# A two-layer strided convolution with a joint head on one core: a new schedule for the leading 254 columns

## Chip, cores, metric

The kernel runs on one core of one Trainium2 chip. The metric is device time of one execution in microseconds (us), median over several executions. The span that the profile shows is about 1.8 us shorter than the time that the same execution reports. Every run in this document was in the fast state. All kernels gave a correct result.

Ratios are computed as the mean time of one kernel's runs over the mean time of the other's runs of the same rounds, so they are not quite the ratio of the medians that are quoted beside them.

## The reference

```python
B, T, D, K = 2, 4000, 512, 5;  U = 8          # all bfloat16
xp = pad(x, 2 columns of zeros at both ends of T)
h = gelu(sum_i xp[:, i:i+T, :] @ w1[i])[:, ::2, :]        # layer 1, 5 taps, stride 2
hp = pad(h, 2 at both ends)
f = gelu(sum_i hp[:, i:i+T1, :] @ w2[i])[:, ::2, :]       # layer 2, 5 taps, stride 2
fe = f @ w_f;  ge = g @ w_g
j = tanh(fe[:, :, None, :] + ge[:, None, :, :])
return j @ w_o                                            # (2, 1000, 8, 512)
```

## The kernel before

Columns are split into four phases (column modulo 4), so both parities of a strided output read whole phases. Layer 1 of batch 0 is cut into three tiles: a leading tile (columns 0 to 249), tile 1 (250 to 499) and tile 2 (500 to 999, 500 wide). Every tile has four groups of 128 output channels, m = 0 to 3. A "tap" is one of the five convolution weights.

The leading tile is computed tap by tap: 5 taps x 4 groups x 2 parities x 4 contraction steps = 160 matmuls. All other tiles use minimal filtering: seven products (b2, a1, a2, a0, b1, b3, a3) of *transformed* operands give both parities, 28 matmuls a group in place of 40. The price is work on other engines: ScalarE copies a phase shifted by one column, VectorE subtracts and adds phases and sums weights (wsum), and each group has a post-processing, a "post" below (ScalarE scales one bank, VectorE combines, ScalarE applies gelu).

```python
CELL = 32            # bytes; dependencies are tracked per cell of this size
...
def xf(src, off, dst, c0, n, which):                  # transforms on VectorE
    ph = lambda r: src[r, :, off:off + n]
    o = lambda kind: dst[kind, :, c0:c0 + n]
    if which == "a0":   tt("dve", o(0), o(0), ph(2), sub)  # o(0): ScalarE's shifted copy
    elif which == "a3": tt("dve", o(2), o(2), ph(0), sub)
    elif which == "b1": tt("dve", o(3), o(3), ph(1), sub)
    elif which == "b3": tt("dve", ph(3), ph(3), ph(1), sub)      # in place
    elif which == "a1": tt("dve", o(1), ph(0), ph(2), add)
    elif which == "a2": tt("dve", ph(0), ph(2), ph(0), sub)      # in place
...
count = {"unit": 2}
...
    def banks(self, m):                               # PSUM: 8 banks of 512 columns
        if self.n <= 256:                             # two banks a group
            base = (count["unit"] % 4) * 2 * NT
            ...
        else:                                         # four banks a group
            base = (count["unit"] % 2) * 4 * NT
            ...
        count["unit"] += 1
...
for i in (0, 4, 2, 1, 3):                             # leading tile, all by taps
    for m in range(NK):
        for s in range(2):
            r, d = tap_at[i][s]
            mm(ps.cols(m * NT + 256 * s, n),
               [(w1_sb[i, k, m*P:(m+1)*P], xs[0][r, k, 16+d:16+d+n]) for k in range(NK)], ...)
for m in range(NK):
    wsum04(w1_sb, w1_t, "dve", m)
wsum13(w1_sb, w1_t, "dve")
...
for w in ("a0", "b1", "a3"):                tiles[1].shift(w)   # ScalarE
for w in ("a0", "b1", "b3", "a3", "a1", "a2"): tiles[1].xf(w)   # VectorE
...
for qi in range(1, len(tiles)):
    ...
    for m in range(NK):
        where = tile.products(m)
        ...
        if qi == 6 and m == 0:
            ge()                                      # small gate product, PSUM bank 0
            fe(0)
```

`CELL` belongs to the program's own planner, not to the chip: the planner makes an engine wait wherever two accesses touch the same cell.

The loads: x for the leading tile (two blocks, "turned", that is transposed, on TensorE) and then transposing loads on SyncE's queue, the five weight taps on ScalarE's queue.

## Time and profile before

| | before |
|---|---|
| time, median of the first three runs | 292.46 us (292.26 to 292.56) |
| time of the run that was profiled | 293.93 us |
| TensorE busy | 280.4 of 292.1 us (96%) |
| chain that ended last | 92% TensorE |
| VectorE, ScalarE busy | 62%, 54% |

TensorE is the bottleneck, so what counts is where it stands still or runs slowly. The waits view of the kernel before lists who kept TensorE waiting (total us, times, longest us):

```profile
PE acc L302 <- DVE ty_67 L291: 2.6, 1, 2.6
PE acc L302 <- DVE xt_54 L291: 2.0, 1, 2.0
PE acc L302 <- POOL warm L288: 1.3, 1, 1.3
PE acc L302 <- DVE ty_69 L291: 1.3, 1, 1.3
PE acc L302 <- issue: 1.2, 1, 1.2
```

The second and the first line are the gaps before tile 1 (27.2 to 29.2 us) and before tile 2 (43.0 to 45.6 us). The timeline of the same kernel shows what was happening in them; the columns are start, duration, engine, line, operation, output and inputs, shape, count, and in brackets the idle time just before and what ended it:

```profile
27.33 0.68 DVE L291 TENSOR_TENSOR xs_49<-xs_49 128x1000 bf16<-128x1000 bf16 x1 [6.99 <-PE acc L302]
...
29.25 1.00 PE L302 MATMUL acc<-xs_49,w_t 128*128 128x250 bf16 x4 [2.02 <-DVE xt_54 L291]
...
43.78 1.19 DVE L291 TENSOR_TENSOR xs_50<-xs_50 128x2000 bf16<-128x2000 bf16 x1
44.89 0.67 DVE L291 TENSOR_TENSOR ty_67<-ty_67,acc 128x500 f32<-128x500 f32 x1
...
45.62 1.15 PE L302 MATMUL acc<-xs_50,w_t 128*128 128x500 bf16 x4 [2.58 <-DVE ty_67 L291]
```

VectorE stood idle for 7.0 us until the last tap matmul was done; then it did three transforms and tile 1 could start. Before tile 2, TensorE waited for the end of VectorE's sum into ty_67, the last post-processing of tile 1.

Windows of 2 us of the same kernel follow: stretch, its length, then busy us and instruction count of TensorE, its weight loads, VectorE, ScalarE and GpSimd, then the granted TensorE clock (1.00 is full speed), the share of the DMA engines and GB/s.

```profile
28.00:30.00 2.00, 0.76 (x4) 0.57 (x5) 1.87 (x4) 0.00 (x0) 0.00 (x0) 0.83 0.95 199
30.00:32.00 2.00, 2.00 (x12) 1.44 (x10) 0.00 (x0) 0.06 (x1) 0.00 (x0) 0.50 1.64 221
...
46.00:48.00 2.00, 2.00 (x7) 0.80 (x6) 0.00 (x0) 0.00 (x0) 0.00 (x0) 0.59 1.22 161
48.00:50.00 2.00, 2.00 (x7) 0.70 (x5) 0.00 (x0) 1.53 (x3) 0.00 (x0) 0.55 1.83 244
```

After each of the two gaps the granted clock falls, to 0.50 in 30 to 32 us and to 0.59 and 0.55 in the two windows from 46 us: TensorE is "busy" all the time, but in 30 to 32 us it starts 12 matmuls of 250 columns where a full-clock window holds about 21.

### The profile page before, as it was taken

The page shows a single profiled execution, that of the slowest core. Times are in us where ns is not written, and L with a number is a line of the kernel's source. Part 1 is how long each engine was busy: PE and PEld are TensorE (multiplying, and loading weights), DVE is VectorE, ACT ScalarE, POOL GpSimd, SP SyncE. Part 2 cuts the span into 40 slices and gives each one's busy share as a digit, 9 for nine tenths or more (in the row PEclk, how much of TensorE's full clock was granted, in tenths as well). Part 3 has the DMA queues.
Part 4 walks back from the last instruction along what each step waited for, and adds up shares of the span by engine and source line. Part 5 has one row for each costly group of instructions (what it writes and reads, how often), then busy time and mean ns, then how long its engine had stood idle before and what let it go on. Part 6 is the DMA issues. An engine that isn't in the chain of part 4 may idle for free.

```text
span 292.1 us, 3892 instructions
## 1 busy us (share of the span) xinstructions
PE 280.4 (96%) x1460; PEld 141.6 (48%) x1460; DVE 182.3 (62%) x237; ACT 158.0 (54%) x187; POOL 33.1 (11%) x39
## 2 busy tenths in 40 slices
PE   8897987999999999999989999999999999999995
PEld 3796873444444444444434444444444444444442
DVE  0872493687598668576633346566757576666764
ACT  2333653722842662563315628667886785975930
POOL 1000000099994000000000000000000000000000
PEclk9999797999999999999999999999999999999999
DMA  7999939990000000000000002244454444444444
GB/s 267 320 205 222 208 74 164 319 312 0 3 0 0 0 2 0 0 2 0 0 0 2 0 1 74 68 147 161 142 167 145 156 151 154 153 148 159 145 148 138
DMA packets 54575, 31.85 MB, mean 109 GB/s; under 512 B 31630, under 2 KB 54302, under 8 KB 54558
## 3 DMA queue, kind: packets, MB, share of 16 engines
q1 hardware_dynamic: 51918, 28.99, 36.6%
q10 hardware_dynamic: 2640, 2.62, 2.7%
q8 instruction: 11, 0.18, 0.3%
q14 instruction: 6, 0.05, 0.1%
HBM read 7.86 MB, written 16.38 MB: 83 GB/s over the span
## 4 chain that ended last, share of the span: by engine, by line
PE 92%; DVE 3%; issue 2%; ACT 1%; POOL 0%; DVEq 0%; ACTq 0%; POOLq 0%
PE acc L302 92%; ACT xt_55 L295 1%; DVE ty_69 L291 1%; PE acc L363 1%; DVE xt_54 L291 0%; DVE xt_55 L291 0%; DVE ty_68 L486 0%; DVE ost_86 L626 0%; DVE ty_67 L291 0%; DVE ty_68 L291 0%; DVE ty_69 L486 0%; DVE ty_67 L486 0%; POOL zero L288 0%; ACT cs_65 L295 0%; ACT cs_66 L295 0%
## 5 line engine op out<-in xcount | busy, mean ns | idle before, releaser
L302 PE MATMUL acc<-wo_sb,jT 128*128 128x512 bf16 x500 | 108.2, 379 | 0.0
L302 PEld LDWEIGHTS acc<-wo_sb,jT 128*128 128x128 bf16 x500 | 48.9, 98 | 59.0
L302 PE MATMUL acc<-xt_55,w_sb 128*128 128x500 bf16 x160 | 38.3, 374 | 0.0
L295 ACT ACTIVATE jT<-feT_80,geT 128x1000 bf16<-128x1000 f32 (+6 forms) x44 | 35.8, 890 | 0.0
L295 ACT ACTIVATE jT<-feT_79,geT 128x1000 bf16<-128x1000 f32 (+4 forms) x40 | 35.1, 949 | 0.0
L302 PE MATMUL acc<-xt_54,w_sb 128*128 128x500 bf16 (+1 forms) x160 | 33.8, 347 | 0.0
L295 ACT ACTIVATE cs_65<-acc 128x500 f32<-128x500 f32 (+1 forms) x12 | 6.6, 553 | 37.8 <-PE acc L302 37.8
L302 PE MATMUL acc<-xs_49,w_sb 128*128 128x250 bf16 (+1 forms) x192 | 23.7, 278 | 1.2 <-issue 1.2
L302 PEld LDWEIGHTS acc<-xt_55,w_sb 128*128 128x128 bf16 x160 | 15.7, 98 | 18.4 <-issue 0.5
L302 PEld LDWEIGHTS acc<-xt_54,w_sb 128*128 128x128 bf16 x160 | 16.0, 100 | 13.4
L302 PEld LDWEIGHTS acc<-xs_49,w_sb 128*128 128x128 bf16 x192 | 18.6, 97 | 4.8 <-issue 1.3
L295 ACT ACTIVATE cs_66<-acc 128x500 f32<-128x500 f32 (+1 forms) x12 | 6.6, 552 | 25.2 <-PE acc L302 25.2
L302 PE MATMUL acc<-xs_49,w_t 128*128 128x250 bf16 (+1 forms) x64 | 13.6, 339 | 2.0 <-DVE xt_54 L291 2.0
L295 ACT ACTIVATE ost_93<-acc 128x512 bf16<-128x512 f32 x10 | 6.0, 597 | 16.4 <-PE acc L302 16.4
L626 DVE CAST ost_82<-acc 128x512 bf16<-128x512 f32 x11 | 7.6, 691 | 10.3 <-PE acc L302 10.3
L626 DVE CAST ost_88<-acc 128x512 bf16<-128x512 f32 x10 | 6.9, 692 | 10.3 <-PE acc L302 10.3
L291 DVE TENSOR_TENSOR ty_69<-ty_69,acc 128x1000 f32<-128x1000 f32 (+1 forms) x8 | 9.0, 1128 | 6.2 <-PE acc L302 6.2
L291 DVE TENSOR_TENSOR ty_68<-ty_68,acc 128x1000 f32<-128x1000 f32 (+1 forms) x8 | 9.0, 1128 | 6.1 <-PE acc L302 6.1
L295 ACT ACTIVATE ost_87<-acc 128x512 bf16<-128x512 f32 x10 | 5.9, 593 | 11.4 <-PE acc L302 11.4
L302 PE MATMUL acc<-xs_50,w_t 128*128 128x500 bf16 x32 | 9.0, 406 | 2.6 <-DVE ty_67 L291 2.6
L291 DVE TENSOR_TENSOR ty_67<-ty_67,acc 128x1000 f32<-128x1000 f32 (+1 forms) x8 | 8.5, 1060 | 4.1 <-PE acc L302 4.1
L486 DVE SCALAR_TENSOR_TENSOR ty_68<-acc,cs_65 128x500 f32<-128x500 f32 x8 | 5.1, 674 | 7.4 <-PE acc L302 7.4
(116 smaller groups left out, 362.4 us busy)
## 6 DMA issues: line engine op xcount, KB each, us to landing
w_sb<-in_w_dram ACTq DMA_DIRECT2D x5, 512.0 KB, 8.4
w_sb<-in_w_dram SPq DMA_DIRECT2D x5, 512.0 KB, 6.4
out_dram<-ost_82 SPq DMA_DIRECT2D x11, 128.0 KB, 1.9
out_dram<-ost_86 SPq DMA_DIRECT2D x11, 128.0 KB, 1.8
out_dram<-ost_84 SPq DMA_DIRECT2D x10, 128.0 KB, 1.8
out_dram<-ost_90 SPq DMA_DIRECT2D x10, 128.0 KB, 1.9
out_dram<-ost_83 SPq DMA_DIRECT2D x9, 128.0 KB
out_dram<-ost_85 SPq DMA_DIRECT2D x9, 128.0 KB
```

Source lines behind the costliest of these rows:

```text
L291: pl.op(eng, lambda e: e.tensor_tensor(out=o.ap, in0=a.ap, in1=b.ap, op=op), (a, b), (o,))
L295: pl.op("act", lambda e: e.activation(o.ap, i.ap, func, scale=scale, bias=0.0 if bias is None else bias.ap), rd, (o,))
L302: ins = e.matmul(o.ap, lhsT=l.ap, rhs=r.ap, start=start and n == 0, stop=stop and n == len(pairs) - 1, skip_group_check=not check)
L363: ins = e.transpose(pv.ap[:, r, k, :], xr[rt].h[:, 2 * pp + r, k, :], ident.h[:, :])
L486: pl.op("dve", lambda e, o=o, f=f: e.scalar_tensor_tensor(out=o.ap, in0=d.ap, scalar=f, in1=c.ap, op0=ALU.mult, op1=add), (d, c), (o,))
L626: pl.op("dve", lambda e, o=o, v=v: e.tensor_copy(out=o.ap, in_=v.ap), (v,), (o,))
```

## The change

As described, it takes the leading columns (254 now) with two channel groups tap by tap and two by minimal filtering; all loads go through one queue, x first, then the taps, then the transposing loads; and the products that read phase 0 come last in the first group of a tile. The core of it, condensed (dots mark cuts, and some lines are joined or commented by me):

```diff
-CELL = 32
+CELL = 4
-    NWARM = 16
+    NWARM = 12
...
-        for i in (0, 4, 2, 1, 3):
-            load_w("act", w1_sb[i], ...)
+        for i in (0, 1, 3, 4, 2):
+            load_w1("sp", i)                 # after the two x blocks, same queue
...                                           # turning: phases 0/2 of both blocks first
+            if which == "a0" and keep:       # leading tile: nothing in place, no shift for a0
+                tt("dve", o(0), src[2, :, off - 1:off - 1 + n], ph(2), sub)
...
-                tt("dve", ph(0), ph(2), ph(0), sub)
+                tt("dve", ph(2), ph(2), ph(0), sub)          # a2 in place in phase 2
...
-        count = {"unit": 2}
+        count = {"unit": 0}
...
+        NA = 254
+        LATE0 = ("a0", "b1", "b3", "b2", "a1", "a2", "a3")
...
+        for w in ("a0", "a1", "a2", "b3"):  t0.xf(w)
+        for w in ("b1", "a3"):  t0.shift(w); t0.xf(w)
+        wsum13(w1_sb, w1_t, "dve")
+        wsum04(w1_sb, w1_t, "dve", 2)
+        wsum04(w1_sb, w1_t, "dve", 3)
+        for i in (0, 1, 3):  direct(i)       # taps, groups 0 and 1
+        filt("a0", "b1");  direct(4);  filt("b3", "a3");  direct(2)
+        filt("b2", "a1", "a2")               # filtering, groups 2 and 3
...                                           # then tile 1's transforms, wsum04 of 0 and 1,
...                                           # gelu of groups 0, 1 and posts of groups 2, 3
-                where = tile.products(m)
+                where = tile.products(m, *((LATE0,) if qi < 3 and m == 0 else ()))
...
+                if qi == 4 and m == 1:
+                    ge()                     # in the bank of the coming unit
                 if qi == 6 and m == 0:
-                    ge()
+                    nbank[0] = (count["unit"] % 2) * 4      # f projection: idle half first
                     fe(0)
...                                           # last output tile in two halves of 256 columns
```

## The prediction

> **What bounds it now.** TensorE: 96% busy (busy shares), 92% of the chain of waits. Granted clock 1.0 nearly everywhere. The waits view has five TensorE waits: 1.3 us at the start, 1.2 before the taps, 2.0 before tile 1 (27.2 to 29.2 us), 2.6 before tile 2 (43.0 to 45.6), 1.3 before the small gate product (147.9 to 149.1). After the 2.0 and 2.6 us gaps, the one-microsecond windows show clock 0.50 for about 3.4 us and 3.9 us: 20 matmuls of 250 columns ran at half rate (about 1.5 us lost) and 10 of 500 columns took 0.42 instead of 0.21 us (2 us lost). After the 1.2 and 1.3 us gaps the clock stayed at 1.0. The Trainium skill ("TensorE: Matmul & The Clock Gate", Part 1) says K/N halves after an idle window of about 3.4 us, free-running; here 2.0 us of idleness was already enough. So the early phase wastes about 4.6 us idle plus 3.5 us cold.
>
> **What the change does.**
> 1. Leading tile: 160 tap matmuls (0.107 us each, 17.3 us) become 136 of 254 columns (est. 0.108, so 14.7): -2.5 us, all on the chain.
> 2. Start: x goes ahead of the taps in one queue, 12 warm-up matmuls instead of 16, and phases 0/2 of both halves are turned first, copied by VectorE. Before, xr_64 landed at about 7.4 us while sharing with taps; 1 MB alone at the 290-400 GB/s of the windows lands near 5.2. Warm-ups end near 5.9, turning of the first phases near 6.9, two 0.69 us copies end near 8.0: first tap at 8.0, not 9.9: -1.9 us. Taps follow at about 1.5 us each (last near 13), ahead of their use.
> 3. The 2.0 us gap and its cold stretch: tile 1's operands and weight sums are now made during the leading tile. I expect no wait over 0.5 us: -3.5 us. Leading tile ends near 22.7 (was 27.2), tile 1 near 34.5 (was 43.0).
> 4. Tile 2: bank rotation no longer waits for tile 1's last post-processing, but VectorE/ScalarE become the pace. Summing trace durations (weight sums 1.94 per group, posts 1.4, 500-wide transforms 1.1-1.2, ScalarE shifts 1.8), VectorE, which also inherits two posts of the leading tile, finishes tile 2's last operand (a3) near 42-43. TensorE, ready at 34.5, trickles through tile 2's first group with several waits of 0.3-1.3 us (3 us in all) and ends it near 43.4, against 53.0 before: -9.6 in total from items 1-4. Each gap is short enough to keep the clock, I think; a half-rate stretch would cost 1-2 us.
> 5. The gate product moves to a free bank in tile 4: the 1.3 us wait goes.
> 6. The last tile in halves: -0.3 us.
>
> A detail: the kept a0 subtraction reads one bf16 off alignment. The skill ("VectorE: DVE Perf Modes", Mode 2x_1P) asks for 4-byte alignment; I expect about 1.2 us instead of 0.67 for it (no such case in this trace), absorbed.
>
> **Sum.** 292.5 - 9.6 - 1.25 - 0.3 + about 0.4 for the risk of a cold stretch = 281.8 us.
>
> **Signs.** Right: first tap at about 8 us, leading tile done by 23, no wait before tile 1, waits on VectorE/ScalarE only in tile 2's first group, that group done near 43-44, no wait near 140, clock 1.0 after 6 us. Wrong: first tap after 9; waits for tap loads; clock 0.5 in the 25 to 45 us stretch; tile 1's transposes arriving after 20 us.
>
> **What would make it wrong.** One queue delivering taps or transposes late; a longer VectorE backlog than summed; the clock dropping in the trickle (then about 284-285). If the backlog is shorter, 279.
>
> Chances: faster 0.93, same 0.06, slower 0.01. Range 279.6 to 284.8.

## The result, and the profile after

| | before | after |
|---|---|---|
| median of the first comparison | 292.51 us (292.26 to 293.92) | 281.91 us (281.00 to 282.13) |
| ratio, 95% interval | | 0.9622 (0.9585 to 0.9659) |
| the same two kernels in later rounds | 292.83 us (9 runs) | 281.12 us (5 runs), ratio 0.9602 (0.9578 to 0.9626) |
| TensorE busy | 280.4 of 292.1 us | 273.9 of 280.3 us (98%) |

The waits view of the changed kernel:

```profile
PE acc L298 <- POOL warm L284: 1.3, 1, 1.3
PE acc L298 <- DMA w_sb<-in_w_dram: 1.1, 1, 1.1
PE acc L298 <- DVE xt_55 L287: 0.7, 2, 0.5
PE acc L298 <- DVE xs_50 L287: 0.2, 1, 0.2
```

The gaps of 2.0, 2.6 and 1.3 us are gone. The first line (the wait for the first memset) was there before too. A wait of 1.1 us is for the first weight tap; it stands where the kernel before had its 1.2 us of "issue" (there ScalarE's copies of the turned x ended 0.1 us before the first tap product). 0.9 us are spent waiting for VectorE. The timeline of the changed kernel shows the first tap product, four of VectorE's transforms, begun ahead of it, and tile 2's first group, which now waits for one VectorE transform after the other:

```profile
7.96 2.48 DVE L287 TENSOR_TENSOR xt_55<-xs_49 128x1016 bf16<-128x1016 bf16 x4
...
8.99 5.39 PE L298 MATMUL acc<-xs_49,w_sb 128*128 128x254 bf16 x48 [1.05 <-DMA w_sb<-in_w_dram]
...
31.80 0.74 DVE L499 SCALAR_TENSOR_TENSOR ty_67<-acc,cs_66 128x246 f32<-128x246 f32 x2 [1.42 <-ACT cs_66 L291]
...
39.71 1.02 PE L298 MATMUL acc<-xt_55,w_t 128*128 128x500 bf16 x4 [0.47 <-DVE xt_55 L287]
40.81 1.20 DVE L287 TENSOR_TENSOR xt_55<-xt_55,xs_50 128x2000 bf16<-128x2000 bf16 x1
40.95 1.02 PE L298 MATMUL acc<-xs_50,w_t 128*128 128x500 bf16 x4 [0.22 <-DVE xs_50 L287]
...
42.15 1.00 PE L298 MATMUL acc<-xt_55,w_sb 128*128 128x500 bf16 x4 [0.18 <-DVE xt_55 L287]
```

The windows of the changed kernel over the same early phase, to be held against those of before: the clock is 1.00 in all of them, also where TensorE works in pieces.

```profile
30.00:32.00 2.00, 2.00 (x22) 1.84 (x20) 0.58 (x2) 2.00 (x3) 0.00 (x0) 1.00 1.08 226
38.00:40.00 2.00, 1.53 (x8) 0.57 (x7) 1.97 (x4) 2.00 (x2) 0.00 (x0) 1.00 1.28 210
40.00:42.00 2.00, 1.75 (x8) 0.44 (x6) 2.00 (x3) 0.95 (x2) 0.00 (x0) 1.00 1.24 251
```

To compare many kernels, I cut each profiled span at two instants read from its timeline: the start of the first tap matmul, and the start of the first matmul of tile 2's second group. Up to the first instant the kernel loads and warms up ("start"), between them lie the leading tile, tile 1 and tile 2's first group ("stretch"), and then comes everything else ("rest"). The three add up to the span.

| kernel | start | stretch | rest | median time, us | ratio to before (95%) |
|---|---|---|---|---|---|
| before (the profiled run) | 9.91 | 43.31 | 238.9 | 292.4 to 292.8 | 1 |
| b_warm | 9.54 | 40.41 | 238.9 | 291.16 | 0.9953 (0.9911 to 0.9995) |
| b_cell4 | 9.69 | 39.90 | 238.9 | 290.34 | 0.9922 (0.9880 to 0.9963) |
| b_rot | 9.95 | 39.40 | 238.9 | 288.91 | 0.9901 (0.9867 to 0.9935) |
| b_cell4_rot_ge | 9.83 | 35.97 | 238.9 | 286.64 | 0.9804 (0.9759 to 0.9849) |
| b_four | 9.83 | 35.98 | 237.4 | 285.03 | 0.9738 (0.9713 to 0.9762) |
| a_b2first | 8.90 | 37.93 | 237.3 | 285.19 | 0.9765 (0.9733 to 0.9796) |
| a_alltap | 8.49 | 35.07 | 237.3 | 282.43 | 0.9667 (0.9630 to 0.9704) |
| a_actq | 8.99 | 34.17 | 237.3 | 282.23 | 0.9663 (0.9633 to 0.9693) |
| **after** (first profile) | 8.99 | 34.00 | 237.3 | 281.91 | 0.9622 (0.9585 to 0.9659) |
| after_again | 7.76 | 34.10 | 237.3 | 281.12 | 0.9602 (0.9578 to 0.9626) |
| a_noshift_3g | 8.50 | 34.09 | 237.3 | 281.44 | 0.9605 (0.9582 to 0.9628) |
| a_noshift_alltap | 8.83 | 35.07 | 237.3 | 282.88 | 0.9651 (0.9625 to 0.9677) |
| a_noshift | 7.91 | 32.44 | 237.4 | 279.78 | 0.9562 (0.9523 to 0.9602) |

Names with b_ are edits of the kernel before, names with a_ edits of the changed kernel; each is described below. after_again is the changed kernel unaltered, run once more for comparison. All outputs are right. The verdicts on record ask for 2%: b_rot, b_cell4 and b_warm count as "same" and b_cell4_rot_ge as "unclear", all others as "faster". The intervals exclude 1, that of b_warm only just.

> The changed kernel again, unaltered, for a comparison on the same chip with the next three. Expected 281.0 to 282.2 us. Its first product started at 9.0 us in the first profile because the first tap had only just landed; in the profile without shift copies the same loads let it start at 7.9 us. If that landing varies from run to run, this profile shows a start between 7.9 and 9.0 us.

It started at 7.76 us, just outside the expected range of 7.9 to 9.0 us, after a wait of 0.3 us for the first tap: the landing does vary from run to run.

One caution about the kernel before: its runs fall into three classes. Over 31 timed runs, the mean granted clock was 0.988 in 8 runs (mean 293.9 us), 0.992 to 0.994 in 17 runs (mean 292.6) and 0.998 to 0.999 in 6 runs (mean 290.9). Two half-rate stretches of about 3.6 us cost about 1.2% of the mean clock, one costs 0.6%. So the classes fit two, one and no half-rate stretch per run. The profiled run of before (0.988) belongs to the slowest class; its profile shows both stretches. A reading of that one profile overstates what the average run loses to the clock.

The experiments below fit this. Where the profile shows one large gap left, the number of runs with the lower mean clock (0.992 to 0.994) goes with its length: two of six at 2.1 us (b_rot), five of six at 3.0 us (b_cell4), six of six at 3.2 us (a_b2first). Where no gap is over 1.4 us (b_cell4_rot_ge, b_four), it is none of eleven. The lengths are from one profile each.

### The profile page after: what moved, and what is told of

It is laid out like the page before. It is cut to its first block, busy times and chain, and to the rows that moved or that the text cites. A ratio compares the mean times of both kernels' runs of the same rounds, so it can differ in the third digit from the quotient of the medians.

```text
span 280.3 us, 3870 instructions
## 1 busy us (share of the span) xinstructions
PE 273.9 (98%) x1436; PEld 137.8 (49%) x1436; DVE 188.0 (67%) x250; ACT 160.3 (57%) x191; POOL 30.2 (11%) x39
## 4 chain that ended last, share of the span: by engine, by line
PE 84%; SPq 6%; DVE 5%; issue 2%; ACT 1%; DMA 1%; DVEq 0%
PE acc L298 84%; SPq L330 4%; SPq L316 2%; DMA xs_49<-in_x_dram 1%; ACT xt_55 L291 1%; DVE xs_50 L287 1%; DVE xt_55 L287 1%; DVE w_t L287 1%; DVE ty_68 L499 1%; DVE ty_68 L287 0%; DVE xt_54 L287 0%; SPq L321 0%; DVE ty_67 L499 0%; DVE ty_69 L499 0%; DVE ssum_71 L287 0%
## 5 line engine op out<-in xcount | busy, mean ns | idle before, releaser
L298 PE MATMUL acc<-wo_sb,jT 128*128 128x512 bf16 (+1 forms) x504 | 108.3, 378 | 0.0
L298 PE MATMUL acc<-xt_55,w_sb 128*128 128x500 bf16 (+1 forms) x192 | 42.1, 357 | 0.2 <-DVE xt_55 L287 0.2
L298 PE MATMUL acc<-xt_54,w_sb 128*128 128x500 bf16 (+1 forms) x160 | 33.2, 342 | 0.0
L298 PEld LDWEIGHTS acc<-xt_55,w_sb 128*128 128x128 bf16 x192 | 18.6, 98 | 18.7 <-issue 0.9
L291 ACT ACTIVATE cs_65<-acc 128x500 f32<-128x500 f32 (+2 forms) x13 | 7.0, 538 | 27.3 <-PE acc L298 27.3
L298 PEld LDWEIGHTS acc<-xt_54,w_sb 128*128 128x128 bf16 x160 | 15.6, 98 | 13.0
L291 ACT ACTIVATE cs_66<-acc 128x500 f32<-128x500 f32 (+2 forms) x13 | 7.0, 536 | 21.8 <-PE acc L298 21.7
L298 PE MATMUL acc<-xs_49,w_sb 128*128 128x254 bf16 (+2 forms) x112 | 15.6, 286 | 1.1 <-DMA w_sb<-in_w_dram 1.1
L298 PE MATMUL acc<-xs_49,w_t 128*128 128x246 bf16 (+2 forms) x72 | 13.8, 315 | 0.0
L287 DVE TENSOR_TENSOR ty_68<-ty_68,acc 128x1000 f32<-128x1000 f32 (+2 forms) x9 | 9.7, 1079 | 5.7 <-PE acc L298 5.7
L287 DVE TENSOR_TENSOR ty_67<-ty_67,acc 128x1000 f32<-128x1000 f32 (+2 forms) x9 | 9.7, 1078 | 5.1 <-PE acc L298 5.1
L298 PEld LDWEIGHTS acc<-xs_49,w_sb 128*128 128x128 bf16 x112 | 10.8, 97 | 4.0 <-DMA w_sb<-in_w_dram 1.2
L291 ACT ACTIVATE ost_87<-acc 128x512 bf16<-128x512 f32 x10 | 5.9, 593 | 11.4 <-PE acc L298 11.4
L287 DVE TENSOR_TENSOR ty_69<-ty_69,acc 128x1000 f32<-128x1000 f32 (+1 forms) x8 | 8.5, 1061 | 4.2 <-PE acc L298 4.1
L298 PE MATMUL acc<-xt_55,w_t 128*128 128x500 bf16 (+1 forms) x48 | 10.0, 341 | 0.5 <-DVE xt_55 L287 0.5
L679 DVE CAST ost_86<-acc 128x512 bf16<-128x512 f32 (+1 forms) x12 | 7.7, 646 | 2.6 <-PE acc L298 2.6
```

The lines of the kernel that those rows point to most:

```text
L287: pl.op(eng, lambda e: e.tensor_tensor(out=o.ap, in0=a.ap, in1=b.ap, op=op), (a, b), (o,))
L291: pl.op("act", lambda e: e.activation(o.ap, i.ap, func, scale=scale, bias=0.0 if bias is None else bias.ap), rd, (o,))
L298: ins = e.matmul(o.ap, lhsT=l.ap, rhs=r.ap, start=start and n == 0, stop=stop and n == len(pairs) - 1, skip_group_check=not check)
L679: pl.op("dve", lambda e, o=o, v=v: e.tensor_copy(out=o.ap, in_=v.ap), (v,), (o,))
```

## The experiments

Theory: most of the gain comes from ending TensorE's stops, and those were caused by small things: a false dependency (CELL), bank rotation (unit, nbank). Rivals: the named parts do it, that is fewer matmuls through filtering, or the new load order.

### b_rot: the bank counter alone

```diff
-        count = {"unit": 2}
+        count = {"unit": 0}
```

> Kernel before, only the bank counter starts at 0 instead of 2, so that tile 2's first group uses banks of tile 1's groups 0 and 1. Theory (the 2.6 us wait before tile 2 is for the last post-processing of tile 1, because of the bank rotation; the half-rate stretch after it is the gap's doing): the wait shrinks to under 0.5 us, since the transforms it also needs were done at 44.9 us and the group starts with products that need less; clock stays 1.0 after 43 us; time falls by 4 to 4.5 us to about 288. Rival (tile 2 waited for VectorE's transforms anyway): the wait only changes its releaser and time falls by less than 1 us.

Measured: 288.91 us, ratio 0.9901, so -2.9 us against the mean of before. First a line of this kernel's timeline (tile 2's third product), then one of its windows:

```profile
45.13 1.00 PE L302 MATMUL acc<-xs,w_t 128*128 128x500 bf16 x4 [0.34 <-issue]
```

```profile
46.00:48.00 2.00, 2.00 (x11) 0.95 (x10) 1.83 (x3) 2.00 (x3) 0.00 (x0) 1.00 1.48 176
```

The 2.6 us wait became 0.34 us and the clock stayed at 1.00 after 43 us; in the profiles the stretch is 3.9 us shorter. The mechanism held. The timed gain was smaller than expected because the average run of before has one half-rate stretch, not the two of its profile. In two of the six runs of b_rot the clock was 0.994 (290.05 us), in the other four 1.0 (288.5 to 289.0).

### b_cell4: the dependency cell alone

```diff
-CELL = 32
+CELL = 4
```

> Kernel before with only the dependency cell changed from 32 to 4 bytes (the constant CELL). Theory (the 2.0 us gap before tile 1 is a false dependency: tile 1's in-place b3 starts at column 266, byte 532, in the same 32-byte cell as the last columns that the taps read, so VectorE waited 7.0 us for the taps' end): VectorE's transforms run during the taps, tile 1 follows the taps without a gap, no half-rate stretch at 29 to 33 us, everything after it 3.5 us earlier; the gap before tile 2 stays: time about 288.5, -3.5 us. Rival (the gap is the weight sums' or the transposes' lateness, as the prediction put it, so only the new order of work closes it): unchanged within 0.5 us.

Measured: 290.34 us, ratio 0.9922. The timeline of this one-constant kernel shows tile 1's first product at 26.84 us without a wait, and the gap before tile 2, now the only large one:

```profile
26.84 0.59 PE L302 MATMUL acc<-xs,w_t 128*128 128x250 bf16 x4
...
38.36 0.59 PE L302 MATMUL acc<-xt,w_sb 128*128 128x250 bf16 x4
41.99 1.47 PE L302 MATMUL acc<-xs,w_t 128*128 128x500 bf16 x4 [3.04 <-DVE ty L291]
```

In this kernel VectorE's in-place b3 runs at 20.3 us, while the taps last until 27.0 us. The gap before tile 1 was a false dependency. Tile 1's in-place b3 writes from column 266, byte 532, which shares a 32-byte cell with the columns up to 265 that the taps read; no byte is shared. The rival as it was put falls: a new order of work was not needed to close this gap. (Whether the new order would close it too is taken up below.) The gap before tile 2 grew from 2.6 to 3.0 us. The stretch lost 3.4 us in the profiles, but the times fell by 2.3 us: the profiled run of before has two half-rate stretches where its average run has one, and five of six runs of b_cell4 had the clock of one.

### b_cell4_rot_ge and b_four: small edits together, no filtering

b_cell4_rot_ge has both edits above, and the gate product in tile 4 in the coming unit's bank. b_four adds:

```diff
         if qi == 6 and m == 0:
+            nbank[0] = (count["unit"] % 2) * 4
             fe(0)
...
-            return (nbank[0] % 8) * NT
+            return ((nbank[0] - 1) % 8) * NT
...
+        nbank[0] = (count["unit"] % 2) * 4          # again, ahead of the output tiles
```

> Kernel before with three small edits: cells of 4 bytes, bank counter from 0, the gate product in tile 4 and in the coming unit's bank. No minimal filtering in the leading tile, no new load order, old product order, 16 warm-ups. Theory (most of the gain is the removal of the three waits and their two half-rate stretches): about 283.5 to 284.5, -8 to -9 us, that is four fifths of the whole gain. Rival (the named parts, filtering and load order, bring the gain): under -6 us.

> Kernel before with cells of 4 bytes, bank counter from 0, gate product in tile 4, and also the bank base of the f projection set to the idle half, as in the change. The version without this last edit still had a 1.3 us wait. Theory: that wait was for the bank of the previous group, not for the gate product's place in the program; it goes and the time falls from 286.6 to about 285.3 us, -7 us against before. Rival (the wait is for something else): stays at 286.6.

Measured: 286.64 us (0.9804, -5.7 us) and 285.03 us (0.9738, -7.7 us). The first missed its expectation of -8 to -9 us and stayed under -6, which was the rival's side; b_four decides between them. Part of the reason is the clock classes again (1.7 us on average, not 3.5); the rest is that a 1.3 us wait stayed, now near 141 us. Moving the gate product only moved the wait to the next product, because the f projection also began in a bank that tile 6's first group still held. With the last edit the wait went and the rest fell from 238.9 to 237.4 us, as expected. Together, four small edits without filtering, load order or product order bring 7.7 of the 11.7 us (1 - 0.9602, times 292.8 us) measured in the same rounds.

### b_warm: useless matmuls in the gaps

```diff
+        keep_warm(7, 8)          # 8 matmuls of zeros, 512 columns, bank 7, after the taps
...
+                keep_warm(4, 10) # 10 more, bank 4, before tile 2
```

> Kernel before with useless matmuls of zeros in its two gaps: 8 of 512 columns after the taps, 10 before tile 2, in banks nobody needs. They end before the real work's operands are ready. Theory (the half-rate stretches are caused by TensorE's idleness and cost about 3.5 us of the gain): both waits keep their length for the real work, the clock stays 1.0 from 6 us on, and the time falls by 2.5 to 3.5 us. Rival (the clock's drop is not due to the idleness, or the products after it were held up otherwise): unchanged within 0.5 us.

Measured: 291.16 us, ratio 0.9953 (upper end 0.9995): -1.4 us. Two of its windows, where before had 0.50 and 0.59:

```profile
30.00:32.00 2.00, 2.00 (x22) 1.83 (x20) 1.14 (x3) 1.63 (x2) 0.00 (x0) 1.00 1.21 209
46.00:48.00 2.00, 2.00 (x11) 0.92 (x10) 1.22 (x3) 2.00 (x3) 0.00 (x0) 1.00 1.70 209
```

All windows taken up to 52 us show clock 1.00, tile 2's first group ran at 0.21 us a matmul, and all six runs have a mean clock of 0.998 or more, against 6 of 31 of before. So TensorE's idleness causes the half-rate stretches. The timed effect was under the expected 2.5 to 3.5 us. Against the classes of before it agrees: the mean of the 31 runs (292.6 us) is 1.7 us above the class with no half-rate stretch (290.9). That number, not the 3.5 us read from one profile, is what the clock was worth.

### a_alltap and a_noshift_alltap: what filtering is worth

The leading tile is computed by taps for all four groups, its transforms and posts are removed, and the weight sums and taps are reordered to suit; the rest is kept (24 more matmuls of 254 columns). The second version also has no shift copies (see below).

```diff
-            for m in (0, 1):
+            for m in range(NK):            # direct(i)
...                                         # filt, t0.xf, t0.shift, t0.post removed
```

> Changed kernel with the leading tile tap by tap for all four channel groups (160 matmuls of 254 columns instead of 136), its transforms and two posts gone, everything else kept. Theory (after the change VectorE paces tile 2's first group, so fewer matmuls are worth less than their TensorE time): TensorE gets 24 x 0.108 = 2.6 us more work, but VectorE loses about 6 us of work before tile 2, the waits in tile 2's first group vanish, and the time rises by only about 1 us, to about 283. Rival (TensorE-bound throughout; the filtering is worth its matmuls): rises by 2.6 us to about 284.5. If the filtering was the main gain of the change (about 10 us), the time would return towards 290.

> Changed kernel without ScalarE's shift copies and with the leading tile tap by tap for all four groups. Theory (filtering was worth only 0.5 us because VectorE and ScalarE paced tile 2; without shift copies TensorE paces everything): the 24 extra matmuls now cost their full 2.6 us, about 282.3 against 279.8 us. Rival (filtering is worth 0.5 us whatever the pace): about 280.3.

Measured: a_alltap 282.43 us, 0.5 to 1.3 us slower than the changed kernel's two medians; its stretch is 35.07 against 34.0 to 34.1 us. TensorE has no wait at all in it after the start. Without shift copies the comparison is 282.88 against 279.78 us, and 35.07 against 32.44 us: 2.6 us in the stretch, the full price of the matmuls. (The times are from different rounds and their profiles start 0.9 us apart, so the stretch is the cleaner figure.) So filtering saves 2.6 us of TensorE time, of which the changed kernel realised only about 1.0 us; the other 1.6 us turned into slower progress in tile 2's first group, where VectorE and ScalarE set the pace.

### a_actq: the taps on the other queue

```diff
-            load_w1("sp", i)
+            load_w1("act", i)
...                                         # ScalarE's warm-up activation moves behind these loads
```

> Changed kernel with the five tap loads issued from ScalarE's queue, as in the kernel before, order of taps kept. Theory (one queue delays the taps: the first tap's landing, not the turning of x, set the first product at 9.0 us): first tap lands near 6 to 7 us, x lands near 7.4 us as before the change, turning starts at about 7.5, first product at about 9.5: time +0.5 us. If one queue is worth nothing and only the order of the instructions counts: first product within 0.2 us of 9.0 and the time unchanged. Either way under 1 us: the queue is not the cause of the 10 us.

Measured: 282.23 us, ratio 0.9663. x landed later (TensorE waited 0.7 us for it at 7.5 us; in the first profile of the changed kernel x had landed by 5.3 us), the first tap earlier (5.9 against 8.9 us), and the first product came at 8.99 us, exactly as in that profile. Whichever is better, the difference is within the spread of the start: seven profiles with unaltered loads show the first product between 7.76 us (after_again) and 8.99 us (after). The Trainium skill ("Trainium Kernel Development and Optimization", Key Constraints) says that queues of different engines feed the same 16 DMA engines and only save issue time; this run agrees. What makes the first tap land at 7.7 us in one run and at 8.9 us in another stays open. The tap is not the only thing that moves: the same 12 warm-up matmuls took 4.4 to 5.3 us in these seven profiles, and where they took 5.3 us turning began only at 6.4 us.

### a_b2first: the old order of products

```diff
-                where = tile.products(m, *((LATE0,) if qi < 3 and m == 0 else ()))
+                where = tile.products(m, *())
```

> Changed kernel with the old order of products (b2, a1, a2, a0, b1, b3, a3) in the first group of tiles 1 and 2. Theory (the late order spreads the wait for VectorE over several short gaps that keep the clock up): tile 1 must wait for the weight sum and a1 (about 23 us): 0 to 0.5 us; tile 2 runs b2 at 35.5 to 36.4 and then stands about 3 us until a1 at 39.7, the clock falls to 0.5 for about 3.5 us; time rises by 3 to 5 us. Rival (the order of products is worth nothing, since the last operand a3 arrives at 42.0 in any case): rises by under 1.5 us.

Measured: 285.19 us, 3.3 and 4.1 us above the changed kernel's two medians. Tile 1 needed no late order. Tile 2 did: the timeline and windows of this run show one gap of 3.2 us and then the half clock. First the timeline, then one window:

```profile
39.64 1.02 PE L298 MATMUL acc<-xt,w_t 128*128 128x500 bf16 x4 [3.18 <-DVE xt L287]
```

```profile
42.00:44.00 2.00, 2.00 (x7) 0.68 (x6) 1.96 (x4) 1.45 (x2) 0.00 (x0) 0.50 1.01 181
```

The late order does not bring the last operand any earlier. It gives TensorE other products to do until then, so that one long gap becomes three of at most 0.5 us, and the clock stays up. Of the 3.9 us by which the stretch grew, part is idleness and part is half rate.

### a_noshift: no shift copies on ScalarE

```diff
-            act(dst[kind, :, c0:c0 + n], src[r, :, off + d:off + d + n], ACT.Copy)
+            del r, d, kind
...
-                tt("dve", o(0), o(0), ph(2), sub)
+                tt("dve", o(0), src[2, :, off - 1:off - 1 + n], ph(2), sub)
```

(and likewise for b1 and a3)

> Changed kernel with ScalarE's shift copies removed everywhere: VectorE's subtractions a0, b1, a3 read the neighbour column directly, 2 bytes off alignment, as the kept a0 already does. Theory (an odd bf16 offset costs a subtraction nothing, as the kept a0 took 0.68 us like its aligned neighbours): the 500-wide ones stay at 1.19 us, ScalarE loses 3 x 1.86 us per tile, VectorE's 1.4 us wait for ScalarE at 30.4 us vanishes, tile 2's first group waits less than 0.4 us: time -0.7 to -1.2 us. Rival ([...]a misaligned operand halves the rate): the 500-wide subtractions take about 2.2 us and the time rises by 1 us or more.

Measured: 279.78 us (279.28 to 280.17), ratio 0.9562, the fastest of all. The rival was what the prediction had expected of the alignment. A subtraction whose first input starts 2 bytes off a 4-byte boundary takes as long as the aligned one, as these lines of VectorE's timeline show (a0 and b1 of tile 2; the second is followed by the aligned in-place b3):

```profile
29.74 1.19 DVE L287 TENSOR_TENSOR xt<-xs 128x2000 bf16<-128x2000 bf16 x1
...
32.07 1.19 DVE L287 TENSOR_TENSOR xt<-xs 128x2000 bf16<-128x2000 bf16 x1
33.30 1.20 DVE L287 TENSOR_TENSOR xs<-xs 128x2000 bf16<-128x2000 bf16 x1
```

The waits view of the same kernel has one line left for TensorE, the memset at the start:

```profile
PE acc L298 <- POOL warm L284: 1.3, 1, 1.3
```

In the changed kernel VectorE had waited 1.42 us at 30.4 us for ScalarE, which was copying a shifted phase (1.86 us) ahead of the scaling that VectorE needed. With the copies gone VectorE runs through, the transforms a1, a2 and a3 are ready 0.3 to 1.0 us before their products, and the stretch is 1.6 us shorter. This version and the changed kernel were timed in different rounds; their runs do not overlap (279.3 to 280.2 against 280.9 to 282.1 us).

### a_noshift_3g: one group more by filtering

Groups 1, 2, 3 by filtering, only group 0 by taps, no shift copies, and the weight sums of group 0 on GpSimd.

```diff
-        base0 = {2: 4 * NT, 3: 6 * NT}
+        base0 = {1: 2 * NT, 2: 4 * NT, 3: 6 * NT}
...
+        wsum04(w1_sb, w1_t, "dve", 1)
         wsum04(w1_sb, w1_t, "dve", 2)
         wsum04(w1_sb, w1_t, "dve", 3)
+        wsum04(w1_sb, w1_t, "pool", 0)
```

> Attempt at a faster version: no shift copies, three channel groups by minimal filtering and one by taps (12 matmuls fewer, 1.3 us), and the weight sums of the tap group on GpSimd. If TensorE paces and VectorE keeps up: 278.6 us, -1.2 against the version without shift copies. If VectorE, which gets one more post and has no idle time between 24 and 46 us, becomes the pace: waits of 0.5 to 2 us in tile 2's first group and no gain. If GpSimd's sums slow VectorE's subtractions, their 1.19 us grows.

(The diff also gives the sums of groups 0 and 1 buffers of their own.)

Measured: 281.44 us, 1.7 us slower than a_noshift (other rounds) in spite of 12 matmuls less; its stretch is 1.65 us longer. TensorE waited 1.3 us for a weight sum. VectorE's and GpSimd's timelines of this run show why the sum was late:

```profile
13.28 1.52 DVE L424 TENSOR_SCALAR w_t<-w_t 128x2048 bf16<-128x2048 bf16 x1
14.72 1.64 DVE L288 TENSOR_TENSOR ssx<-w_sb 128x512 f32<-128x512 bf16 x1
...
18.45 0.68 DVE L288 TENSOR_TENSOR ssum<-w_sb 128x512 f32<-128x512 bf16 x1
```

```profile
12.28 1.97 POOL L288 TENSOR_TENSOR ssx<-w_sb 128x512 f32<-128x512 bf16 x1 [10.32 <-DMA w_sb<-in_w_dram]
14.33 3.04 POOL L288 TENSOR_TENSOR w_t<-ssx,w_sb 128x512 bf16<-128x512 f32 x2
```

While GpSimd worked, the doubling of the weight sum took 1.52 us and the sum of two taps 1.64 us; alone they take 0.69 us (in a_noshift) and 0.68 us (the third line). The Trainium skill ("GPSIMD Engine Reference", 1. Specifications) names the SBUF interfaces as shared with VectorE, with contention when a VectorE instruction has two SBUF inputs or runs in a 2-port mode. This trace agrees and gives the size: more than twice as slow. The attempt failed in a way near the third of its expected outcomes, though the instructions that grew were the weight sums and not the 1.19 us subtractions. It is not the whole loss: TensorE also stood 0.5 us after the first tap, and tile 2's first group took 0.7 us longer than in a_noshift, as in the second outcome.

## Why the prediction was right, and where its sum was not

The predicted time (281.8 us) and the direction were right. Point by point:

- **The stretch before the second group of tile 2, item 1 to 4: -9.6 us predicted, -10.2 us in the first pair of profiles** (53.22 to 42.99 us), -11.4 us in the second. The total held, but its parts did not.
- **Item 1, "-2.5 us, all on the chain", failed.** The TensorE time was right (2.6 us, a_noshift against a_noshift_alltap). What it is worth was not: without filtering (a_alltap) tile 2's first group has no wait at all, so filtering brings the time down by only 0.5 to 1.3 us. Item 4 charged the waits separately and did not see that they were the price of item 1.
- **Item 2, start: -1.9 us predicted, -0.9 and -2.2 us in two profiles.** x landed at 5.3 us as estimated. That the taps would be "ahead of their use" failed for the first one: it was the limit, with waits of 1.1 and 0.3 us.
- **Item 3, the gap before tile 1: gone, as predicted, but the reason given was not what had opened it.** I put it down to operands and sums being made during the leading tile. b_cell4 closes it with one constant. Which of the two closes it in the changed kernel is not shown, since none of the runs has the new order with cells of 32 bytes. By the code, cells of 32 bytes would make tile 1's b3 wait there for taps 0, 1 and 3, and a2 for the last tap product; in the first profile these end at 14.4 and 21.3 us, and b3 and a2 start at 19.7 and 23.0 us. So the new order probably closes the gap as well. The 7.0 us that VectorE stood idle "for TensorE" were on the page, and I did not ask which bytes that dependency was about.
- **The half-rate stretches, 3.5 us, were mis-sized.** They were read from one run of the slowest class. On average they cost 1.7 us (31 runs of before), and b_warm, which removes them and nothing else, gained 1.4 us.
- **Item 4: bank rotation and the trickle: right.** b_rot isolates the rotation. TensorE lost 1.5 to 1.6 us in tile 2's first group, not the 3 us predicted: VectorE's last operand was ready at 42.0 us as summed (42 to 43), while TensorE came to tile 2 1.0 us later than predicted. The clock stayed at 1.0, and a_b2first shows that this was owed to the order of products.
- **Item 5, -1.25 us: right in size**, 1.5 us by b_four. But it was the bank base of the f projection that removed the wait; the gate product's new place alone only moved it. Whether the bank base alone would do was not tried.
- **Item 6, the last tile in halves, -0.3 us: not seen.** b_four without halves and the changed kernel have the same rest, 237.4 and 237.3 us.
- **The detail on alignment: wrong.** a0 took 0.68 us, not 1.2.

So the predicted total is right partly by luck, because errors offset each other: about 1.8 us too much for the clock (3.5 against 1.7 us) stands against 1.4 us too much for the waits in tile 2's first group (3 against 1.6 us) and 0.4 us added for a cold stretch.

Of the 11.7 us of the last comparison, b_four accounts for 7.7 us. The remaining 4.0 us are, in its profile and that of after_again, 2.1 us of earlier start and 1.9 us of shorter stretch: about 1.0 us from filtering and 0.9 us from the other reorderings (b_four 35.98, a_alltap 35.07 us). Which of the start's parts (12 warm-ups, the order of turning, the order of loads) brings the 2.1 us was not tried one by one.

## What to carry to other kernels

When an engine waits for another one "to finish", ask which bytes or which bank the wait is about. Two of the three large gaps here were a dependency cell that was too coarse and a PSUM rotation that returned to the bank written last, and both close with one number. Take a saving in matmuls as a gain only after checking that the engine which prepares their operands is not the pace; here about 1.6 of 2.6 us became visible only when ScalarE's copies were removed. And look at several runs before costing a clock effect from one profile.

## What the Trainium skill lacked or had wrong

- "TensorE: Matmul & The Clock Gate", Why this matters for your kernels, advises against idle gaps over about 3 us. Here gaps of 2.0 and 2.6 us were followed by clock 0.50 in the profiled run; by the mean clock, 25 of 31 runs had at least one half-rate stretch and 6 had none. Gaps of 1.2 and 1.3 us left the clock at 1.0. What the page lacks is the price of a single gap under its window: about 1.5 us in some runs and nothing in others, in two of six runs with a gap of 2.1 us and in five of six with one of 3.0 us.
- "VectorE: DVE Perf Modes", Mode 2×_1P, asks for 4-byte alignment. "Vector Engine (DVE) Microarchitecture Reference", 5.1, says that alignment makes no difference. The runs side with the latter: 1.19 us with and 1.20 us without misalignment at 2000 elements a partition, 0.68 us at 1016.
- "GPSIMD Engine Reference", 1. Specifications, names the contention but gives no size; another page of the skill says more on who waits for whom, so it is only the size that is added. Here two VectorE instructions on bf16 in SBUF took 1.52 in place of 0.69 us and 1.64 in place of 0.68 us while GpSimd worked.
- No page gives how far the landing of one and the same load moves from run to run: the first 512 KB tap, issued at 1.63 us behind 1 MB of x, landed at 7.7 and at 8.9 us in two profiles of the same kernel.
